# Turning q by the DMA crossbar instead of TensorE and VectorE

## The chip, the cores and the metric

The kernel runs on one core of one Trainium2 chip. The metric is the device time of one execution in microseconds (us). An execution more than 1.5% above the fastest of the same kernel counts as slow. Ratios use the fast ones alone; medians are over all executions.

SBUF is the memory on the chip that holds the tiles; PSUM, divided into banks, takes the results of TensorE here. DMA engines move data beside the computing engines, in packets. The granted clock is the share of TensorE's full clock that the profile reports.

## The reference, cut to what matters

```python
kv  = einsum('bhsd,bhse->bhde', k, v)            # per batch b and head h: 64 x 64
out = einsum('bhsd,bhde->bhse', q, kv)           # q: (8, 8, 576, 64)
out = out / sqrt(mean(out**2, -1) + 1e-6) * g_norm
x   = out.transpose(0, 2, 1, 3).reshape(4608, 512)
h   = x @ w_in                                   # (512, 1024)
solu = h * softmax(h)
ln  = (solu - mean) / sqrt(var + 1e-6) * g_ln    # over the 1024
result = ln @ w_out                              # (1024, 512)
```

`q @ kv` contracts over d, the last dimension of q. A matmul contracts over partitions, so q, which arrives with tokens on the partitions, has to be turned first. This turn is what the change is about.

## The kernel before

The work is cut into nine chunks of 512 tokens: chunks 0 to 7 hold 512 tokens of one batch each, chunk 8 the last 64 of all eight. Each engine gets a fixed order of instructions. A small list scheduler (`Plan.order`) finds it at build time: every piece of work is entered with its engine, an assumed length and its needs, and at each step the piece that could start first is taken. No order is written by hand.

The parts concerned (cuts are marked `...`):

```python
def load_q(b):                       # GpSimd's queue, casts f32 to bf16
    t = T["q", b] = tile_of(("q", b), [128, H, 4, D], BF16)
    nc.gpsimd.dma_start(...)

def qT_mm(c, hf, tag):               # half a chunk: 8 transposes into a PSUM bank
    t = T["qTp", c, hf] = bank((tag,), [128, 4, 2, 128], BF16)
    for h in range(4):
        for y in range(2):
            src = T["q", c][:, 4 * hf + h, 2 * y:2 * y + 2, :].rearrange("p z d -> p (z d)")
            nc.tensor.transpose(t[:, h, y, :], src, ident[:, :])

def qT_copy(c, hf):                  # and its evacuation
    t = T["qT", c, hf] = tile_of(("qT", c, hf), [128, 4, 2, 128], BF16)
    nc.vector.tensor_copy(t[:, :, :, :], T["qTp", c, hf][:, :, :, :])
...
def o_mm(c, hf, tag): ...            # o = kv' q', needs the turned q
def e_sum(c, n):                     # GpSimd: sum of two exponential tiles, 1.27 us
    ...
    nc.gpsimd.tensor_tensor(out=T["es", c][:, n, :], in0=e[:, 0, :], in1=e[:, 1, :], op=ADD)
...
def stats(c):                        # mean and variance of a chunk; tiny tiles
    nc.vector.tensor_copy(st[:, :, :], T["st", c][:, :, :])                       # from PSUM
    nc.vector.tensor_tensor(out=sq[:, :, :], in0=st[:, :, 1:3], in1=st[:, :, 1:3], op=MUL)
    nc.vector.tensor_tensor(out=var[:, :], in0=st[:, :, 0], in1=sq[:, :, 0], op=SUB)
    nc.vector.scalar_tensor_tensor(out=T["vare", c][:, :], in0=sq[:, :, 1], scalar=..., in1=var[:, :], op0=MUL, op1=ADD)
```

After o come its squares, their mean per head, logarithm and exponential, the product x, then h = x w_in (`h_ps` in the profile), u = h exp(h), the sums for the statistics, and the output matmuls (`out_ps`), which are scaled (`ob_sb`) and stored from SyncE's queue.

The softmax here doesn't subtract the row's maximum and nothing guards it: scores larger than these inputs give would overflow.

## Time and profile before

| | before |
|---|---|
| time, median (us) | 222.2 (4 runs, 220.6 to 223.0; 221.6 by the three known at the prediction) |
| span of the profiled execution | 218.7 |
| first h matmul | 23.15 |
| q of chunk 0 and 1 turned, first use in an o matmul | 15.18 and 30.34 |
| a steady chunk (from one chunk's turn of the sums to the next) | 19.90 |

TensorE is the fullest engine from 55 us on; before that, loads fill the DMA engines. The lines are in the prediction below. One more view, the time order of TensorE around the first use of the turned q in chunks 0 and 1 (start, us, engine, line, operation; in brackets the idle time before it and what ended it):

```profile
15.18 0.29 PE L274 MATMUL o_ps<-qT_sb,kvd 64*64 64x256 bf16 x1 [0.51 <-DVE kvd L247]
```

### The profile page before, as it was taken

How to read it: one execution, taken by the hardware profiler on the slowest of the kernel's cores; microseconds unless marked ns; L12 is line 12 of the kernel's file. 1: busy time of each engine (PE TensorE's matmuls, PEld its weight loads, DVE VectorE, ACT ScalarE, POOL GpSimd, SP SyncE). 2: the span in 40 equal slices, each digit the busy share in tenths (PEclk: the TensorE clock that was granted, in tenths of full speed). 3: DMA queues.
4: the chain of work that ended last, by engine and by line, in shares of the span. 5: the costliest groups of instructions: out<-in, count | busy, mean ns of one | idle time of the engine just before them, and what ended most of it. 6: DMA issues, size and time to landing. Idle time of an engine off the chain costs nothing.

```text
span 218.7 us, 4197 instructions
## 1 busy us (share of the span) xinstructions
PE 188.8 (86%) x1669; PEld 85.8 (39%) x1695; DVE 137.7 (63%) x249; ACT 133.8 (61%) x227; POOL 131.8 (60%) x136
## 2 busy tenths in 40 slices
PE   7669796588999989999998999899999999999900
PEld 2434343243553444344435444443453444344300
DVE  1326564896777596669648675966785675493240
ACT  2019577757866877784977679586849685342000
POOL 8606299529479727984695584468466477485000
PEclk9699999999999999999999999999999999999995
DMA  5999999994992697289719940311032022013023
GB/s 53 187 201 205 230 361 201 201 189 53 201 210 60 94 193 185 63 109 221 190 13 189 224 115 4 109 48 51 0 119 76 3 96 96 0 64 125 6 69 124
DMA packets 30483, 27.01 MB, mean 123 GB/s; under 512 B 2304, under 2 KB 24832, under 8 KB 30464
## 3 DMA queue, kind: packets, MB, share of 16 engines
q0 software_dynamic: 24112, 17.30, 52.1%
q1 hardware_dynamic: 6352, 9.44, 12.6%
q8 instruction: 13, 0.21, 0.4%
q14 instruction: 6, 0.05, 0.1%
HBM read 32.51 MB, written 9.44 MB: 192 GB/s over the span
## 4 chain that ended last, share of the span: by engine, by line
PE 63%; DVE 14%; ACT 9%; DMA 5%; issue 4%; POOL 1%; DVEq 1%; POOLq 0%; ACTq 0%
PE out_ps L487 24%; PE h_ps L365 23%; PE misc_ps L429 6%; DMA v_sb<-in_v_dram 5%; PE misc_ps L257 3%; PE s_ps L295 3%; PE o_ps L274 3%; DVE u_sb L380 3%; DVE x_sb L310 2%; DVE ob_sb L494 2%; DVE kvd L247 2%; DVE w_out_sb L478 2%; ACT lss_sb L299 2%; ACT e_sb L373 2%; ACT osq_sb L289 2%
## 5 line engine op out<-in xcount | busy, mean ns | idle before, releaser
L365 PE MATMUL h_ps<-x_sb,w_in_sb 128*128 128x512 bf16 x273 | 71.7, 379 | 5.1 <-DVE x_sb L310 3.1
L391 POOL TENSOR_TENSOR usq_sb<-u_sb 128x512 bf16<-128x512 bf16 x58 | 59.9, 1040 | 23.1 <-DVE u_sb L380 23.1
L373 ACT ACTIVATE e_sb<-h_ps,zero_t 128x512 f32<-128x512 f32 x72 | 49.2, 684 | 37.7 <-PE h_ps L365 35.7
L487 PE MATMUL out_ps<-w_out_sb,u_sb 128*128 128x512 bf16 x262 | 67.1, 380 | 2.4 <-DVE ob_sb L494 1.1
L397 POOL TENSOR_TENSOR es_sb<-e_sb 128x512 bf16<-128x512 f32 x36 | 45.7, 1269 | 37.4 <-ACT e_sb L373 37.3
L380 DVE TENSOR_TENSOR u_sb<-h_ps,e_sb 128x512 bf16<-128x512 f32 x72 | 48.9, 684 | 22.9 <-ACT e_sb L373 22.6
L365 PEld LDWEIGHTS <-w_in_sb 128*128 128x128 bf16 x288 | 26.4, 98 | 34.7 <-issue 7.7
L487 PEld LDWEIGHTS <-u_sb 128*128 128x128 bf16 x288 | 26.1, 98 | 34.5 <-issue 7.0
L494 DVE TENSOR_SCALAR ob_sb<-out_ps,rstd 128x512 f32<-128x512 f32 x34 | 24.9, 743 | 11.7 <-PE out_ps L487 10.2
L310 DVE SCALAR_TENSOR_TENSOR x_sb<-o_ps,g_rep,rst_sb 128x512 bf16<-128x512 f32 x34 | 25.4, 746 | 6.5 <-ACT rst_sb L303 6.4
L303 ACT ACTIVATE rst_sb<-lss_sb,zero_t 128x512 f32<-128x512 f32 x36 | 25.8, 722 | 0.6
L299 ACT ACTIVATE lss_sb<-s_ps,eps_t 128x512 f32<-128x512 f32 x34 | 23.2, 683 | 1.9 <-PE s_ps L295 1.9
L289 ACT ACTIVATE osq_sb<-o_ps,zero_t 128x512 bf16<-128x512 f32 x33 | 21.1, 684 | 3.7 <-PE o_ps L274 2.7
L249 ACT CAST kvd<-misc_ps 64x256 bf16<-64x256 f32 x16 | 5.9, 368 | 16.7 <-DVE kvd L247 16.3
L295 PE MATMUL s_ps<-osq_sb,head_mean 128*128 128x512 bf16 x34 | 12.9, 380 | 0.7 <-ACT lss_sb L299 0.7
L257 PE MATMUL misc_ps<-ident,q_sb 128*128 128x128 bf16 x120 | 9.5, 224 | 3.8 <-DMA q_sb<-in_q_dram 2.0
L257 PEld LDWEIGHTS <-q_sb 128*128 128x128 bf16 x128 | 8.8, 103 | 8.8 <-issue 3.5
L438 DVE STREAM_TRANSPOSE sumT_sb<-misc_ps 128x512 f32<-128x512 f32 x9 | 6.4, 713 | 9.1 <-PE misc_ps L429 9.1
L261 DVE COPY qT_sb<-misc_ps 128x1024 bf16<-128x1024 bf16 x17 | 11.6, 679 | 0.4 <-PE misc_ps L257 0.4
L389 ACT ACTIVATE usq_sb<-u_sb,zero_t 128x512 bf16<-128x512 bf16 x14 | 10.1, 722 | 2.6 <-DVE u_sb L380 2.6
L274 PE MATMUL o_ps<-qT_sb,kvd 64*64 64x32 bf16 (+1 forms) x248 | 8.7, 229 | 2.2 <-DVE kvd L247 1.1
L247 DVE CAST kvd<-misc_ps 64x256 bf16<-64x256 f32 x16 | 6.6, 414 | 5.3 <-PE misc_ps L238 3.0
(60 smaller groups left out, 133.0 us busy)
## 6 DMA issues: line engine op xcount, KB each, us to landing
out_dram<-ob_sb SPq DMA_DIRECT2D x36, 256.0 KB, 3.1
k_sb<-in_k_dram POOLq DMA_DIRECT2D x8, 576.0 KB, 7.3
v_sb<-in_v_dram POOLq DMA_DIRECT2D x8, 576.0 KB, 9.8
q_sb<-in_q_dram POOLq DMA_DIRECT2D x8, 512.0 KB, 12.6
w_out_f<-in_moe_w_out_dram POOLq DMA_DIRECT2D x1, 2048.0 KB, 26.1
w_in_sb<-in_moe_w_in_dram POOLq DMA_DIRECT2D x2, 512.0 KB, 13.8
q_last<-in_q_dram POOLq DMA_DIRECT2D x8, 64.0 KB, 3.1
g_rep<-in_g_norm_dram SPq DMA_DIRECT2D x2, 0.2 KB, 2.3
```

Of the source, the lines that this page charges most:

```text
L257: nc.tensor.transpose(t[:, h, y, :], src, ident[:, :])
L289: nc.scalar.activation(out=t[:, :], in_=T[("o", *i)].rearrange("p a b c -> p (a b c)"), func=AF.Square, bias=zero_t[:, :])
L299: nc.scalar.activation(out=t[:, :], in_=T["s", i][:, :], func=AF.Ln, bias=eps_t[:, :])
L303: nc.scalar.activation(out=t.rearrange("p a b c -> p (a b c)"), in_=T["lss", i][:, :], func=AF.Exp, scale=-0.5, bias=zero_t[:, :])
L310: nc.vector.scalar_tensor_tensor(out=T["x", c][:, 2 * hf:2 * hf + 2, z], in0=T["o", c, hf, z][:, :, :, :], scalar=g_rep[:, :], in1=T["rst" ...
L365: nc.tensor.matmul(t[:, :], w_in_sb[:, dt, f * 128:(f + 1) * 128], T["x", c][:, dt].rearrange("p a b c -> p (a b c)"), start=(dt == 0), st ...
L373: nc.scalar.activation(out=T["e", c, f // 2][:, f % 2, :], in_=T["h", c, f][:, :], func=AF.Exp, bias=zero_t[:, :])
L380: nc.vector.tensor_tensor(out=T["u", c][:, f, :], in0=T["h", c, f][:, :], in1=T["e", c, f // 2][:, f % 2, :], op=MUL)
L391: nc.gpsimd.tensor_tensor(out=dst, in0=src, in1=src, op=MUL)
L397: nc.gpsimd.tensor_tensor(out=T["es", c][:, n, :], in0=e[:, 0, :], in1=e[:, 1, :], op=ADD)
L487: nc.tensor.matmul(T["acc", c, m][:, :], T["u", c][:, f, m * 128:(m + 1) * 128], w_out_sb[:, f, :], start=(f == 0), stop=(f == NF - 1),)
L494: nc.vector.tensor_scalar_mul(out=t[:, :], in0=T["acc", c, m][:, :], scalar1=T["rstd", c][:, m:m + 1])
```

## The change

The intent is to free TensorE, the fullest engine, of 144 transposes and VectorE of 18 copies, by letting the DMA engines turn q from SBUF to SBUF. The core of the diff:

```diff
-            done[n] = t + length + (0.2 if engine == "pe" else 0.12)
+            done[n] = t + length + {"pe": 0.2, "sp": 1.5}.get(engine, 0.12)
...
-    plan.add("warm2", "pe", 2.6, -9.0, lambda: warm(12), [("qT_mm", 0, 1)], first=[("s", "warm2")])
+    plan.add("warm2", "pe", 5.2, -8.0, lambda: warm(24), ["warm"], first=[("s", "warm2")])
...
-    def qT_mm(c, hf, tag): ...
-    def qT_copy(c, hf): ...
+    def q_turn(c):
+        t = T["qT", c] = tile_of(("qT", c), [128, H, 2, 128], BF16)
+        nc.sync.dma_start_transpose(
+            t.rearrange("q h y p -> q (h y) p"), T["q", c].rearrange("p h j d -> p (h j d)")
+        )
...
+        plan.add(("qT", c), "sp", 2.2, r, lambda c=c: q_turn(c),
+                 [("q", c)] if c < B else [("q_last", b) for b in range(B)], ...)
```

The schedule is told that a turn takes 2.2 us on SyncE and is there 1.5 us later.

More of the change, by code (lines that the diff above doesn't have):

```diff
@@ L113 @@
     bufs = {
-        "k": 3, "v": 3, "q": 3, "qT": 4, "osq": 4, "lss": 2, "rst": 2, "oc": 2, "x": 2, "e": 4, "u": 2, "usq": 2, "es": 2,
+        "k": 3, "v": 3, "q": 3, "qT": 2, "osq": 4, "lss": 2, "rst": 2, "oc": 2, "x": 2, "e": 4, "u": 2, "usq": 2, "es": 2,
         "sumT": 2, "ob": 4,
@@ L249, in kv_copy @@
             nc.scalar.copy(dst, src)
-    def qT_mm(c, hf, tag):
-        t = T["qTp", c, hf] = bank((tag,), [128, 4, 2, 128], BF16)
-        for h in range(4):
-            for y in range(2):
-                src = T["q", c][:, 4 * hf + h, 2 * y:2 * y + 2, :].rearrange("p z d -> p (z d)")
-                nc.tensor.transpose(t[:, h, y, :], src, ident[:, :])
-    def qT_copy(c, hf):
-        t = T["qT", c, hf] = tile_of(("qT", c, hf), [128, 4, 2, 128], BF16)
-        nc.vector.tensor_copy(t[:, :, :, :], T["qTp", c, hf][:, :, :, :])
+    def q_turn(c):
[3 more added lines that the diff above has]
+        )
     def o_mm(c, hf, tag):
@@ L275, in o_mm @@
                             ts[z][hh * 64:hh * 64 + 64, pp, :, cols], kvd[rows, b, hh, 2 * hf + pp, :],
-                            T["qT", c, hf][rows, 2 * pp + hh, :, cols], start=True, stop=True,
+                            T["qT", c][rows, 4 * hf + 2 * pp + hh, :, cols], start=True, stop=True,
                         )
@@ L326 @@
         kvs = [("kv", b, hh, z) for b in ([c] if c < B else range(B)) for hh in range(2) for z in range(2)]
+        plan.add(("qT", c), "sp", 2.2, r, lambda c=c: q_turn(c),
+                 [("q", c)] if c < B else [("q_last", b) for b in range(B)],
+                 uses=[("q", c)] if c < B else [], first=[("qT", c)])
         for hf in range(2):
-            loads = [("q", c)] if c < B else [("q_last", b) for b in range(B)]
-            qtag = "h" if c == 0 and hf else "misc"
-            plan.add(("qT_mm", c, hf), "pe", 0.5, (r + w * (0.1 + 0.1 * hf)) if c else -2.0, lambda c=c, hf=hf, tag=qtag: qT_mm(c, hf, tag),
-                     ["ident", *loads], uses=[("q", c)] if c < B else [], first=[(qtag, "qT", c, hf)])
-            plan.add(("qT", c, hf), "dve", 0.62, (r + w * (0.12 + 0.1 * hf)) if c else -2.0, lambda c=c, hf=hf: qT_copy(c, hf),
-                     [("qT_mm", c, hf)], uses=[(qtag, "qT", c, hf)], first=[("qT", c, hf)])
             tag = "out" if c == 0 and hf else "o"
             plan.add(("o_mm", c, hf), "pe", 0.25 if c < B else 1.2, r + w * (0.35 + 0.5 * hf),
-                     lambda c=c, hf=hf, tag=tag: o_mm(c, hf, tag), [("qT", c, hf), *kvs],
-                     uses=[("qT", c, hf)], first=[(tag, c, hf, z) for z in range(2)])
+                     lambda c=c, hf=hf, tag=tag: o_mm(c, hf, tag), [("qT", c), *kvs],
+                     uses=[("qT", c)], first=[(tag, c, hf, z) for z in range(2)])
             for z in range(2):
```

## The prediction

> **What bounds the kernel now.** I read the engine totals first, then the 40 slices, then the chain that ended last, then the groups of the lines that the change touches, and last the chain inside one steady chunk.
>
> The totals and three rows of the slices (each slice is 5.47 us; a digit is tenths busy):
>
> ```profile
> PE 188.8 (86%) x1669; PEld 85.8 (39%) x1695; DVE 137.7 (63%) x249; ACT 133.8 (61%) x227; POOL 131.8 (60%) x136
> ...
> PE   7669796588999989999998999899999999999900
> ...
> DMA  5999999994992697289719940311032022013023
> ```
>
> TensorE is the fullest engine, and its row is at 8 or 9 from slice 11 (55 us) to slice 38. Before that it is at 5 to 9, while the DMA row is at 9. So there are two stages: a head of some 50 us, in which loads and latencies set the pace, and a long stage where TensorE does. The change must be judged in each.
>
> The chain that ended last, by engine, agrees:
>
> ```profile
> PE 63%; DVE 14%; ACT 9%; DMA 5%; issue 4%; POOL 1%; DVEq 1%; POOLq 0%; ACTq 0%
> ```
>
> Of this the turning of q on TensorE (line 257) has 2.7%, by the chain's list of lines: 0.027 x 218.7 = 5.9 us. These are the groups that go (mean ns of one, then idle before them):
>
> ```profile
> L257 PE MATMUL misc_ps<-ident,q_sb 128*128 128x128 bf16 x120 | 9.5, 224 | 3.8 <-DMA q_sb<-in_q_dram 2.0
> ...
> L261 DVE COPY qT_sb<-misc_ps 128x1024 bf16<-128x1024 bf16 x17 | 11.6, 679 | 0.4 <-PE misc_ps L257 0.4
> ```
>
> And this is the chain in the middle of one steady chunk (start, us, what), from the chunk that runs from 111.65 to 131.55 us:
>
> ```profile
> 118.36 0.43 DVE kvd L247
> 118.79 0.02 issue
> 118.81 0.38 ACT kvd L249
> 119.19 0.04 issue
> 119.23 0.61 PE misc_ps L257 x8
> 119.84 0.86 PE h_ps L365 x4
> 120.70 0.86 PE out_ps L487 x4
> 121.57 0.45 PE misc_ps L257 x8
> ```
>
> The reader is to see two things here. Eight transposes advance the chain by 0.45 us (56 ns each), although one is listed with 219 to 224 ns: they are pipelined, so their busy time is not their cost. And the first eight wait for the last evacuation of k'v (line 249). They write the "misc" bank, of which there is one, which k'v, both halves of the turned q and the sums of the statistics share. In the time order TensorE is idle 0.48 us before 119.23 for this.
>
> **What the skill says.** "TensorE: Matmul & The Clock Gate", "Wait — 56ns, not 53.3ns?", has 55.6 ns from start to start at N = 128 with a warm clock; the trace agrees (0.45 / 8 = 56 ns). "VectorE: DVE Perf Modes", "The three transpose paths", gives 1309 ns for one 128x128 bf16 tile by the DMA crossbar. "DMA: Bandwidth & Descriptors", "Latency and other measured facts", gives a transposing DMA 261 GB/s where the middle dimension is not contiguous, and 350 to 400 where it is. The kernel before has no such DMA, so its trace can't decide between them, and they are far apart for one turn of 128x2048 (512 KB, sixteen such tiles): 524,288 B / 261 GB/s = 2.0 us, but 16 x 1.309 = 20.9 us if tiles went one by one. The same page, "Queues, rings and completion order", says each DMA engine goes round-robin between queue rows, packet by packet. The trace fits: a 256 KB store on the SyncE queue lands in 3.1 us (median) and 6.4 at worst, amid loads that take 7 to 13.
>
> **The change, part by part.**
>
> 1. *TensorE loses 144 transposes* (9 chunks x 16). Per chunk 16 x 56 ns = 0.90 us of issue time. With it goes the 0.48 us wait for the "misc" bank, if nothing else fills that place: sums and k'v come at other times of the chunk. So 0.9 to 1.4 us per chunk where TensorE is the bound. That holds for the chunks whose q is turned after 55 us: chunks 3 to 7 and the last one (line 257 near 60, 80, 99, 119, 139 and 157 us), six in all. 6 x 0.9 = 5.4 and 6 x 1.4 = 8.3; I take 7 us. The steady chunks last 19.9 us, with 19.05 us listed as TensorE busy, 13.9 VectorE, 15.1 ScalarE and 14.5 GpSimd, so no other engine stops a chunk of 18.7.
>
> 2. *VectorE loses 18 copies* of 0.68 us, 12.2 us. In the steady stage it is 70% busy and its copies are beside other work: nothing more. In the head two of them lie in the chain (at 45.0 and 46.9 us, 0.60 each, between the w_out scalings): 1.2 us comes back there.
>
> 3. *SyncE gains nine issues*, one of 2.2 us by the schedule's own figure, with 1.5 us to landing. I take it as an estimate of the author's. The queue has only 36 stores (0.3 us each if nothing blocks them), so 9 x 2.2 us is no load. It is in order, though: a turn that waits for a late q holds up stores behind it. Four output buffers give those stores most of a chunk of slack.
>
> 4. *The DMA engines gain* nine moves of 512 KB inside SBUF. In the steady stage k, v, q and stores take their share for about half of a chunk, and q of chunk 7, issued at 114.3 us, is first used at 139: there is room for a turn of 4 to 8 us. In the head there isn't: asked for 5 to 50 us, the DMA view shows 9 in each slice but the last, and some 200 GB/s. Each of three turns there (chunks 0, 1 and 2) pushes the loads behind it back by its own length, 2.0 to 2.6 us (524,288 B at 261 and at 200 GB/s, an estimate).
>
> 5. *What that costs the head.* q of chunk 0 lands at 7.4 us and its turn would be there at about 11 to 14, while the first use of it is at 15.2, after k'v: not late by itself. But v of chunk 0, whose landing at 13.6 us is in the chain, comes up to 2 us later. q of chunk 1 lands at 28.0, where its first transposes start at once and the first half is turned by 29.5. With a DMA of about 5 us on top and 2 us of delay before, that is 35. The x of chunk 1 (now done at 42.8) doesn't slip by all of this, since ScalarE does the exponentials of chunk 0 in the meantime. w_out lands at 34.5 and would land at 38 to 39. Its eight scalings on VectorE follow, less the 1.2 us of part 2. I put the head at 2 to 3 us longer in all, with the clock warm-up (24 idle matmuls at the start in place of 12 there and 12 later) worth nothing either way.
>
> 6. *Buffers*: two for a whole turned q in place of four halves, the same bytes. A turn waits for the output matmuls of the chunk two before, which are over by then.
>
> Sum: -7 (part 1), -1 (part 2), +2.5 (part 5): about -5.5 us, 221.6 to **216 us** (0.975).
>
> **The rivals.**
> *The turn is slow.* If the tile figure of 1309 ns holds one by one, a turn takes 21 us, longer than a chunk, and the DMA becomes the bound: 9 x 21 = 190 us from the landing of q0, plus a last chunk, some 230 us or more. For it: the page's figure. Against it: that is one lone tile, most of which could be fixed latency, and the schedule's figures (2.2 + 1.5 us) look like measured ones. A milder form, 8 to 12 us when it alternates with loads, stays hidden in the steady stage and costs the head 5 us or more: no gain, 219 to 224.
> *Another wait comes in TensorE's place.* In the steady chunk the chain also runs through statistics, u, ob and k'v on VectorE and ScalarE (114.9 to 119.2 us). If those dependences and not TensorE's issue order set the chunk, the removal gives half: 219 us. Against it: TensorE was busy during that stretch but for the half microsecond before the transposes.
> *The head hides it all.* If v0 slips by nothing and q1 is turned in slack, the full 8 us show: 212 to 213.
>
> **Range and chances.** The middle case is 216. The best, with all of part 1 and a free head, is near 210; the milder slow turn gives 224. The 8-in-10 range is 210 to 225, wider upward since the turn's time is in no trace that I have. Faster by over 2% means under 217.2: 0.54. Within 2%: 0.26. Slower: 0.20, nearly all of it the first rival.
>
> **What would show it.** The profile of the changed kernel should list no line 257 or 261, about 144 fewer matmul records, VectorE busy near 125 us, steady chunks of 18.5 to 19.0 us, nine transposing DMAs with 4 to 8 us to landing, and the first h matmul (now 23.15 us) at 23 to 26. If TensorE waits for the turned q after 60 us, or stores pile up behind a turn, the first rival is right. If chunks stay near 19.9 with no such wait, the second is. The prediction is wrong most simply if landing takes over 10 us.

## More of the kernel before

```profile
30.34 0.41 PE L274 MATMUL o_ps<-qT_sb,kvd 64*64 64x256 bf16 x8
```

Neither waits for q: the first waits for k'v (kvd), the second for nothing.

## The result, and the profile after

The changed kernel takes 243.98 us (median of 4 runs, 242.9 to 246.2), the kernel before 222.17. The ratio is 1.100 (95% interval 1.090 to 1.111): **slower by 10%**. Ratios here are the mean time of one kernel's fast runs over that of the other's in the same rounds, so not quite the ratio of the medians. The result is correct.

The page of the changed kernel: totals, two rows of the 40 slices (6.03 us each), the chain that ended last by engine and by line, and one row of the DMA issues (count, then median us from issue to landing):

```profile
PE 190.7 (79%) x1538; PEld 81.1 (34%) x1563; DVE 130.0 (54%) x231; ACT 133.4 (55%) x227; POOL 131.8 (55%) x136
...
PE   8910787276978799999799899989969799999910
...
DMA  6999999999089956996976997045021103103113
...
PE 51%; DMA 22%; DVE 14%; ACT 4%; issue 3%; POOL 3%; DVEq 1%; POOLq 0%; ACTq 0%
PE out_ps L479 19%; PE h_ps L357 19%; DMA qT_sb<-q_sb 12%; DMA q_sb<-in_q_dram 10%; PE misc_ps L421 5%; DVE u_sb L372 3%; DVE x_sb L305 3%; DVE ob_sb L486 3%; PE o_ps L269 3%; PE s_ps L290 2%; DVE var L448 1%; ACT lss_sb L294 1%; PE misc_ps L238 1%; DVE kvd L247 1%; DVE vare L450 1%
...
qT_sb<-q_sb SPq DMA_TRANSPOSE x8, 4.4
```

The work is gone as planned: no transposes, VectorE 7.7 us less. TensorE's busy time nevertheless rose from 188.8 to 190.7. Two things that the page shows add to it: the warm-up has 12 more idle matmuls (2.6 us), and matmuls are longer while the clock is low (h matmuls 389 ns in the mean, before 379). The first slices of TensorE are emptier, and DMA went from 5% of the chain to 22%: 12% are turns and 10% the load of q of chunk 1. The median landing of 4.4 us looks harmless, and that is the trap: it is the steady stage's. The same views as above, for chunks 0 and 1:

```profile
25.51 0.64 PE L269 MATMUL o_ps<-qT_sb,kvd 64*64 64x256 bf16 x8 [9.64 <-DMA qT_sb<-q_sb]
```

```profile
47.25 0.64 PE L269 MATMUL o_ps<-qT_sb,kvd 64*64 64x256 bf16 x8 [4.41 <-DMA qT_sb<-q_sb]
```

And the chain between them (start, us, what):

```profile
7.45 24.12 DMA q_sb<-in_q_dram
31.57 0.02 issue
31.58 15.62 DMA qT_sb<-q_sb
47.21 0.04 issue
47.25 0.64 PE o_ps L269 x6
```

The turn of chunk 0 was issued at 7.79 us, when its q landed, and was there at 25.5: 17.7 us. The turn of chunk 1 took 15.6, and its q had landed at 31.57, 3.6 us later than before. So the first o matmuls came 10.3 us late, those of chunk 1 16.9 us late. The chain holds the load of q and the turn of chunk 1; the turn of chunk 0 is not in it, since TensorE, done with what that turn had delayed, still idled 4.41 us for chunk 1.

The turn of chunk 2, issued at 48.83 us, still has packets after 58, but TensorE does not wait for it. That of chunk 3 is the third to be waited for. It is in the chain too (first line), and TensorE idled 1.81 us for it (second line):

```profile
70.15 12.80 DMA qT_sb<-q_sb
```

```profile
83.00 0.41 PE L269 MATMUL o_ps<-qT_sb,kvd 64*64 64x256 bf16 x8 [1.81 <-DMA qT_sb<-q_sb]
```

The steady stage did not gain either. These are the windows of one chunk (stretch, its length, then busy us and instructions of TensorE, its weight loads, VectorE, ScalarE and GpSimd, clock, DMA share, GB/s), before and then after:

```profile
111.65:131.55 19.90, 19.05 (x177) 8.76 (x184) 13.91 (x26) 15.12 (x26) 14.53 (x16) 1.00 0.83 146
```

```profile
108.17:128.51 20.34, 18.65 (x162) 7.86 (x168) 13.73 (x24) 15.16 (x26) 14.55 (x16) 1.00 0.95 172
```

TensorE has less to do in the chunk, and the chunk is 0.44 us longer. So there are two questions: what the turns cost in the head, and what ate the gain in the steady stage.

### The profile page after: what moved, and what is told of

The parts are those of the page before. It is cut to its first block, busy times and chain, and to the rows that moved or that the text cites. A ratio compares the mean times of both kernels' runs of the same rounds, so it can differ in the third digit from the quotient of the medians.

```text
span 241.1 us, 3926 instructions
## 1 busy us (share of the span) xinstructions
PE 190.7 (79%) x1538; PEld 81.1 (34%) x1563; DVE 130.0 (54%) x231; ACT 133.4 (55%) x227; POOL 131.8 (55%) x136
## 4 chain that ended last, share of the span: by engine, by line
PE 51%; DMA 22%; DVE 14%; ACT 4%; issue 3%; POOL 3%; DVEq 1%; POOLq 0%; ACTq 0%
PE out_ps L479 19%; PE h_ps L357 19%; DMA qT_sb<-q_sb 12%; DMA q_sb<-in_q_dram 10%; PE misc_ps L421 5%; DVE u_sb L372 3%; DVE x_sb L305 3%; DVE ob_sb L486 3%; PE o_ps L269 3%; PE s_ps L290 2%; DVE var L448 1%; ACT lss_sb L294 1%; PE misc_ps L238 1%; DVE kvd L247 1%; DVE vare L450 1%
## 5 line engine op out<-in xcount | busy, mean ns | idle before, releaser
L357 PE MATMUL h_ps<-x_sb,w_in_sb 128*128 128x512 bf16 x272 | 73.5, 389 | 5.9 <-DVE u_sb L372 3.2
L479 PE MATMUL out_ps<-w_out_sb,u_sb 128*128 128x512 bf16 x264 | 70.3, 390 | 3.5 <-DVE ob_sb L486 2.6
L479 PEld LDWEIGHTS <-u_sb 128*128 128x128 bf16 x288 | 26.9, 99 | 40.4 <-issue 12.9
L486 DVE TENSOR_SCALAR ob_sb<-out_ps,rstd 128x512 f32<-128x512 f32 x34 | 25.2, 745 | 21.0 <-PE out_ps L479 16.9
L269 PE MATMUL o_ps<-qT_sb,kvd 64*64 64x32 bf16 (+1 forms) x248 | 9.7, 238 | 22.2 <-DMA qT_sb<-q_sb 15.9
L290 PE MATMUL s_ps<-osq_sb,head_mean 128*128 128x512 bf16 x34 | 13.7, 404 | 3.0 <-ACT lss_sb L294 2.0
L269 PEld LDWEIGHTS <-kvd 64*64 64x64 bf16 x256 | 4.9, 111 | 29.6 <-issue 22.0
L175 PE MATMUL s_ps<-zeros 128*128 128x512 bf16 x36 | 10.4, 457 | 1.3 <-DVE zeros L145 1.2
L280 POOL TENSOR_TENSOR osq_sb<-oc_sb 128x512 bf16<-128x512 f32 x1 | 1.0, 1038 | 17.8 <-DVE oc_sb L276 17.8
## 6 DMA issues: line engine op xcount, KB each, us to landing
w_in_sb<-in_moe_w_in_dram POOLq DMA_DIRECT2D x2, 512.0 KB, 15.6
```

The lines of the kernel that those rows point to most:

```text
L269: nc.tensor.matmul(ts[z][hh * 64:hh * 64 + 64, pp, :, cols], kvd[rows, b, hh, 2 * hf + pp, :], T["qT", c][rows, 4 * hf + 2 * pp + hh, :, c ...
L357: nc.tensor.matmul(t[:, :], w_in_sb[:, dt, f * 128:(f + 1) * 128], T["x", c][:, dt].rearrange("p a b c -> p (a b c)"), start=(dt == 0), st ...
L479: nc.tensor.matmul(T["acc", c, m][:, :], T["u", c][:, f, m * 128:(m + 1) * 128], w_out_sb[:, f, :], start=(f == 0), stop=(f == NF - 1),)
L486: nc.vector.tensor_scalar_mul(out=t[:, :], in0=T["acc", c, m][:, :], scalar1=T["rstd", c][:, m:m + 1])
```

## The experiments

Theory 1: the turn is slow because it shares the DMA engines with the loads of the head. Rival: the schedule's new order of work is what costs. A kernel has an order (that of before, or that of the change) and a way to turn q (TensorE, DMA, or none at all with a constant tile in its place). Experiments take the two apart. That orders were the same was checked on each computing engine, instruction group by instruction group in the time order, apart from the turning of q and what the table names.

The runs that were timed in several rounds, in one table. "Stats" is the start of VectorE's turn of the sums, one per chunk, a good milestone. The chunk length is from the stats of chunk 3 to those of chunk 4.

| run | order | q turned by | time, us | first h | stats 0 | chunk 3 to 4 | stats 8 |
|---|---|---|---|---|---|---|---|
| before | before | TensorE | 222.7 | 23.15 | 50.69 | 19.90 | 204.75 |
| the change | change | DMA | 244.0 | 33.52 | 63.90 | 20.34 | 227.33 |
| none_after_order | change | none | 225.5 | 25.45 | 49.94 | 20.33 | 210.59 |
| none_before_order | before | none | 217.1 | 25.48 | 52.65 | 18.93 | 201.75 |
| dma_before_order | before | DMA | 234.1 | 33.77 | 69.45 | 18.93 | 218.56 |
| head_by_pe | its own | TensorE 0-3, DMA 4-8 | 227.2 | 25.60 | 54.52 | 20.33 | 211.18 |
| head3_before_order | before | TensorE 0-2, DMA 3-8 | 217.7 | 23.45 | 51.77 | 18.93 | 200.89 |
| only_head_dma | before | DMA 0-1, TensorE 2-8 | 240.6 | 33.33 | 69.57 | 19.90 | 223.64 |
| none_warm | before | none | 215.9 | 23.62 | 50.80 | 18.92 | 199.92 |
| none_after_x_first | change, three pairs swapped | none | 225.5 | 24.52 | 50.71 | 20.33 | 211.36 |
| none_after_psum | change | none | 219.7 | 24.62 | 50.19 | 19.25 | 203.66 |
| after_psum | change | DMA | 241.3 | 34.62 | 64.62 | 19.25 | 225.88 |
| head3_psum | before | TensorE 0-2, DMA 3-8 | 215.7 | 24.91 | 53.38 | 18.93 | 200.15 |

Times are medians; that of before is from the rounds of the first four experiments (in other rounds 221.5 to 223.2). Rounds of different experiments ran on different chips, and the kernel before moved by 1.7 us between them, so differences across rounds are good to 1 or 2 us only. Without their one slow execution head3_before_order is at 217.4 and head3_psum at 215.5. The milestones are from the profiled execution, which for the kernel before was one of its fastest (220.5 us).

### Order and turn, taken apart

```diff
 # none_after_order: the changed kernel, wrong on purpose
+    q_const = big.tile([128, H, 2, 128], BF16, name="q_const")
+    nc.vector.memset(q_const, 0.05)
     def q_turn(c):
-        t = T["qT", c] = tile_of(...); nc.sync.dma_start_transpose(...)
+        T["qT", c] = q_const
```

> The changed kernel with its nine turns taken out and nothing in their place (o is computed from a constant tile, so the result is wrong on purpose); the order of work on every engine is that of the changed kernel, instruction for instruction. Theory 1 (the turn loses its time as a slow DMA among the loads of the head): the first h matmul is back at 22 to 24 us, against 33.5 with the turn, and the time is 211 to 219 us. Rival (the changed order of work costs most of it): the time stays at 230 us or above. Side question: if a steady chunk stays near 20.3 us, as with the turn, the steady stage is set by the order and not by the DMA; if it falls to 18.5 to 19, the DMA holds it.

It took 225.45 us, between the 211 to 219 of theory 1 and the 230 of the rival: each has a part. The head is nearly back (first h at 25.45, expected 22 to 24), but the steady chunk stays at 20.33 us. So the DMA does not hold the steady chunk; the order does.

```diff
 # none_before_order: the kernel before, wrong on purpose
     def qT_mm(c, hf, tag):
-        ... 8 transposes
+        pass
     def qT_copy(c, hf):
-        ... copy
+        T["qT", c, hf] = q_const
```

The scheduler still plans the empty pieces with their old lengths, so all other work keeps its order.

> The kernel before with its transposes and copies of q taken out and nothing in their place (constant tile, wrong on purpose); the order of all other work is that of the kernel before. It shows the most that part 1 and 2 of the prediction could give. If they were right: 212 to 215 us, steady chunks of 18.5 to 19.0 us in place of 19.9. Rival (a chain of dependences through VectorE and ScalarE holds the chunk, not TensorE's issue): 218 us or more, chunks of 19.5 or more.

217.14 us, ratio to before 0.975 (0.969 to 0.982), above the 212 to 215 expected and below the rival's 218. The steady chunk lost 0.97 us, as expected. Part of what is missing is the clock, as shown further below.

```diff
 # dma_before_order: as above, and
+        plan.add(("q_turn", c), "sp", 0.1, r - 1.0, lambda c=c: q_turn(c), ...)   # as soon as q is there
```

> The DMA turn, but with all other work in the order of the kernel before (three turned tiles, the turn issued as soon as q is there). Theory 1: the head loses as in the changed kernel, first h matmul at 32 to 35 us, and the time is 232 to 242 us. Rival (the changed order is what costs): 222 us or less.

234.05 us, ratio 1.051 (1.045 to 1.058), correct. Its steady chunk is the same as without any turn:

```profile
110.84:129.76 18.92, 18.16 (x158) 7.87 (x160) 12.63 (x23) 15.00 (x27) 14.55 (x16) 1.00 1.02 181
```

The whole cost of the turns in this order, 234.05 - 217.14 = 16.9 us, is there by the stats of chunk 0 (69.45 - 52.65 = 16.8) and doesn't grow after.

The four medians now give the account of the change: taking the work away -5.6 us (217.1 - 222.7), the new order +8.3 (225.45 - 217.14), the turns +18.5 (243.98 - 225.45, from different rounds). The milestones of the profiled executions agree in sign and rank at the stats of chunk 8: -3.00 + 8.84 + 16.74 = 22.58 us. The first is smaller there because the profiled execution of the kernel before was one of its fastest.

### Where the turns cost

> Chunks 0 to 3 are turned by TensorE and VectorE as before, chunks 4 to 8 by DMA as in the change; the order is the schedule's own for this mix. Theory 1: without turns among the loads of the head the loss is gone: first h matmul at 23 to 24 us, 215 to 224 us. Rival (the DMA turn costs everywhere, by blocked stores or by a slow steady stage): 228 us or more.

The edit enters the old pieces for chunks 0 to 3 and the new one for 4 to 8 and lets the scheduler find its own order. 227.20 us, ratio 1.022 (1.014 to 1.030). The first h matmul comes at 25.6 (23 to 24 expected), so the head's loss of ten microseconds is mostly gone, but the time is above the range expected: the chunk is again 20.33 us. The expectation had counted the turns and forgotten the order.

> Chunks 0 to 2 turned by TensorE as before, chunks 3 to 8 by DMA, all other work in the order of the kernel before. From the runs so far: the order of before costs nothing, a steady chunk loses 0.97 us by the turn and the head is that of before. Over chunks 3 to 8 this is 5 us: 215.5 to 218.5 us, faster than both kernels. Rival (turns cost something in the steady stage that the runs without them hide): 220 us or more.

```diff
 # head3_before_order: dma_before_order, and
+    HEAD = (0, 1, 2)
     def qT_mm(c, hf, tag):
+        if c not in HEAD:
+            return
         ... 8 transposes                       # likewise qT_copy; o_mm takes either tile
```

217.73 us, ratio 0.977 (0.971 to 0.983), correct, faster than both kernels. Its turns land in 4.5 to 6.0 us, and TensorE waits for none of them. The opposite mix:

> The opposite mix: only chunks 0 and 1, whose turns fall among the loads of the head, are turned by DMA, chunks 2 to 8 by TensorE as before; the order is that of the kernel before. If the head's two turns alone cost what the run with all turns lost against none (16.8 us, with 0.97 us per chunk not won back): 236 to 241 us, first h matmul at 33 to 34 us, steady chunks 19.9 us. Rival (the loss needs the later turns too): below 232 us.

`HEAD = (2, 3, 4, 5, 6, 7, 8)` gives 240.63 us, ratio 1.084 (1.077 to 1.092), with the stats of chunk 0 at 69.57 and the old chunk of 19.90 us. Two turns, those of chunks 0 and 1, are enough for the whole loss of this order: 18.9 us at the stats of chunk 0 (against the run without any turn, which is itself 2.0 us later there than the kernel before, 16.9). No run separates the two; the chain of this one, too, holds the turn of chunk 1 (15.5 us) and not that of chunk 0. In the changed order the turn of chunk 3 comes on top.

### Why a turn in the head is slow

```diff
 # quiet_turn: the changed kernel, in load_q(0)
+        turn_now(0)
+        nc.gpsimd.tensor_copy(held_t[:, :], T["qT", 0][:, H - 1, 1, 127:128])   # GpSimd waits for the turn
```

> The changed kernel, but GpSimd reads one element of the first turned tile before it issues any load other than that of q of chunk 0. So the first turn runs on empty DMA engines, and all later loads start some 9 us later. Theory 1 (a turn is slow only because its packets alternate with those of the loads): the first turn lands 4 to 5 us after its issue, in place of 17.7. Rival (the first turn is slow of itself, or because it is first): it stays above 10 us. The total is no test here, since the loads start late; 236 to 250 us.

The time, one look, was 249.9 us, as the loads start late. The first turn landed in 4.4 us. This is the DMA view of the 4.5 us around it (queue: packets, MB, share of the 16 engines' time; then the issue, us to landing):

```profile
q1 hardware_dynamic: 2080, 0.52, 61.3%
...
qT_sb<-q_sb SPq DMA_TRANSPOSE x1, 4.4
```

And the same turn in the changed kernel, from 8 to 24 us, beside the loads (q0):

```profile
q0 software_dynamic: 3059, 2.56, 100.6%
q1 hardware_dynamic: 2068, 0.50, 24.7%
```

A turn is 2080 packets, 0.52 MB, so some 250 bytes each. Alone they move at some 215 GB/s. Beside the loads they need until 25 us, and the loads move five times as many bytes in the 16 us shown. The turn is not slow of itself; beside the loads it gets a sixth of the bytes.

> The changed kernel with each turn issued as two of half the size (four pairs of heads each), into two tiles. If the turn's packets alternate with the loads' packets one by one, landing grows with the number of packets: the first half of chunk 0 lands 8 to 10 us after its issue and the second near 17.7. If instead the turn stands in a line behind the loads issued before it, both halves land together, at 16 us or later. The time is 238 to 245 us, as x of chunk 0 needs both halves.

Each turn was issued as two halves into two tiles. One look: 237.5 us (state unknown). TensorE's first uses of the halves:

```profile
19.77 0.64 PE L270 MATMUL o_ps<-qTh_sb,kvd 64*64 64x256 bf16 x8 [3.20 <-DMA qTh_sb<-q_sb]
...
26.99 0.64 PE L270 MATMUL out_ps<-qTh_sb,kvd 64*64 64x256 bf16 x8 [6.59 <-DMA qTh_sb<-q_sb]
```

The first half landed 11.9 us after its issue, the second 7.2 us after the first (17.7 after its own issue). So the turn does not stand in one line behind all earlier loads, or both would have come together. Nor is 11.9 within the 8 to 10 us of the other theory: the landing grows with the packets, on top of a few microseconds. I then tried to find the rule by which the engines share.

> The changed kernel, with the first turn run beside a known load: GpSimd issues q of chunk 0, then w_out and w_in with their rows of 2048 bytes as before, and holds all other loads until the turn has landed. From the quiet turn (130 packets on each of 16 engines, some 20 ns each, and 1.8 us fixed) and about 110 ns for a load packet of 2 KB: if the engine takes one packet of the turn and one of the load in turns, 1.8 + 130 x (20 + 110) ns = 18.7 us, less where the loads run out before (96 packets each engine, at 14 us). So 12 to 19 us. Rival (shares by bytes or by time, half each): 7 to 8 us, whatever the packet size.

> The same bytes beside the first turn, but w_out and w_in are read in pieces of 512 bytes, four times as many packets of about a quarter of the time each (some 30 ns). Packet by packet: 1.8 + 130 x (20 + 30) ns = 8.3 us, so 7 to 11 us, clearly less than beside packets of 2 KB. Rival (shares by bytes or time): the same landing time in both runs.

Both let the first turn run beside w_out and w_in alone, in rows of 2048 bytes and in pieces of 512. The landing was 14.2 us and 12.4:

```profile
qT_sb<-q_sb SPq DMA_TRANSPOSE x1, 14.2
```

```profile
qT_sb<-q_sb SPq DMA_TRANSPOSE x1, 12.4
```

The first lies in the range of "one packet each in turns", the second does not (7 to 11), and neither lies at the 7 to 8 us of equal shares. The landing times alone don't give the rule. The packet counts of a stretch in which both queues are at work do. This is the DMA view of the changed kernel from 16 to 20 us, then of the two runs from 16 to 18 us, beside_2k first:

```profile
q0 software_dynamic: 625, 0.62, 91.4%
q1 hardware_dynamic: 625, 0.16, 29.9%
```

```profile
q0 software_dynamic: 318, 0.31, 91.3%
q1 hardware_dynamic: 317, 0.08, 30.1%
...
q0 software_dynamic: 675, 0.17, 82.3%
q1 hardware_dynamic: 676, 0.17, 64.7%
```

One packet of the turn goes with one packet of the loads, whatever its size: the bytes are as one to four where a load packet is counted with 1.0 KB, and equal where it has 250 bytes. Equal shares of the bytes would not give this. A pair takes 102 ns on each of the 16 engines in the changed kernel (4 us / 39), 101 in beside_2k and 47 in beside_512, where 130 and 50 had been assumed.

The second term is the start. Alone the turn's packets begin 1.2 us after its issue (by the slices of the DMA view of quiet_turn). In the changed kernel none is seen before 12 us, over 4 us after it; in beside_2k and beside_512 they begin some 4.5 and 5 us after it. An estimate from these: 4.4 + 130 x 0.102 = 17.7 us, as measured. Why the start is later beside loads stays open; the expectation for beside_512 missed it.

### Why the matmuls of the head were late even with no turn

Without turns the first h matmul still came at 25.5 us, not 23.15. The kernel before had 12 idle matmuls after its transposes, up to 12.7 us; the experiment issues them earlier and then idles until v lands.

> The kernel before without transposes and copies, as in the run with the order of before, but with 34 in place of 12 idle matmuls in the second warm-up, so that TensorE stays busy until v of chunk 0 lands at about 13.6 us. If the first h matmul came at 25.5 us in place of 23.15 only because the clock had fallen in the idle time from 9.5 to 14 us, it is back at 23 to 24 us here and the time is 1.5 to 2.5 us less than 217.1. Rival (something else delays it): no change, 25.5 us and 217 us.

```diff
-    ... lambda: warm(12), [("qT_mm", 0, 1)]
+    ... lambda: warm(34), [("qT_mm", 0, 1)]
```

The k'v matmuls of chunk 0, without and with the longer warm-up:

```profile
14.23 1.49 PE L238 MATMUL misc_ps<-v_sb,k_sb 96*64 96x64 bf16 x48 [4.74 <-DMA v_sb<-in_v_dram]
```

```profile
14.20 0.95 PE L238 MATMUL misc_ps<-v_sb,k_sb 96*64 96x64 bf16 x48
```

The same 48 matmuls take 1.49 us at a granted clock of 0.50 (14 to 15 us) and 0.95 at 1.00. The first h matmul is at 23.62 again and the time 215.91 us (ratio 0.969, 0.965 to 0.974), 1.2 us less than without (a little short of the 1.5 to 2.5 expected). So part of what the transposes did, together with the idle matmuls behind them, was to keep TensorE's clock up.

### What the new order costs in the steady chunk

The chain of a steady chunk in the new order has an x product between u and the first output scaling, which TensorE awaits for 0.85 us. The first idea was this place.

> As the run without turns in the changed order (225.45 us, steady chunk 20.34 us; wrong on purpose), with one pair of VectorE instructions swapped in each of three steady chunks: the x product before the u product after the statistics, so that VectorE does x in the 0.62 us in which it waits for the exponential, as the order of before does. If this place sets the longer chunk, TensorE's wait of 0.85 us for the first ob goes and the three chunks fall by 0.6 to 0.9 us each, the time by about 2 us, to 223.5 us. Rival (the order costs elsewhere, the swap only moves the wait): chunks of 20.2 us or more, no change.

Three pairs were swapped in the order found. Result: 225.50 us, chunks of 20.34 us, no change. The idea fell. VectorE had not been idle before u, as I had taken from the chain's "issue" of 0.62 us; a look at the time order of VectorE and GpSimd (from none_after_order) shows what it did:

```profile
118.84 1.25 DVE L449 SCALAR_TENSOR_TENSOR vare<-sq,var 128x4 f32<-128x4 f32 x1
```

```profile
118.81 1.26 POOL L388 TENSOR_TENSOR es_sb<-e_sb 128x512 bf16<-128x512 f32 x1 [0.57 <-ACT e_sb L364]
```

The last of the small statistics instructions, on 128x4 elements, takes 1.25 us where it usually takes 0.16 (median), and it ends with a GpSimd addition that began 0.03 us before it. The Trainium skill has this: "SBUF — State Buffer", "SBUF: two separate sides", says that VectorE and GpSimd share a port pair as an exclusive lock, which a VectorE instruction with two SBUF inputs needs against a GpSimd instruction that reads SBUF, and that the later one blocks. `vare` reads sq and var, both in SBUF. In the order of before it starts at 114.93 us in its chunk, 0.43 before the GpSimd addition at 115.36, and takes 0.16. The test takes the second SBUF input away:

```diff
-        nc.vector.tensor_tensor(out=sq..., in0=st[:, :, 1:3], in1=st[:, :, 1:3], op=MUL)
+        nc.vector.tensor_tensor(out=sq..., in0=st[:, :, 1:3], in1=T["st", c][:, :, 1:3], op=MUL)
-        var = small.tile([128, 4], FP32, name="var")
+        var = T["st", c][:, :, 0]            # the variance goes back into its PSUM bank
-        nc.vector.tensor_tensor(out=var[:, :], in0=st[:, :, 0], in1=sq[:, :, 0], op=SUB)
+        nc.vector.tensor_tensor(out=var, in0=T["st", c][:, :, 0], in1=sq[:, :, 0], op=SUB)
```

> The run without turns in the changed order (225.45 us, steady chunk 20.34 us; wrong on purpose), with the statistics written so that none of their small VectorE instructions has two SBUF inputs (the variance goes back into its PSUM bank). In that run the last of them took 1.25 us instead of 0.16 in each of three steady chunks, beginning just after the GpSimd addition of 1.26 us began. Theory (the two lock each other out, and the changed order brings them together): the instruction takes 0.2 us everywhere, the steady chunks fall to 19.2 to 19.5 us, the time to 220.5 to 223 us. Rival (the long record only shows another wait): chunks stay at 20.3 us.

The two instructions meet as before, and the small one is short:

```profile
114.39 1.27 POOL L388 TENSOR_TENSOR es_sb<-e_sb 128x512 bf16<-128x512 f32 x1 [0.58 <-ACT e_sb L364]
114.43 0.16 DVE L449 SCALAR_TENSOR_TENSOR vare<-sq,misc_ps 128x4 f32<-128x4 f32 x1
```

The chunk fell to 19.25 us, as expected, and the time to 219.74, 5.7 us less than without this edit by the medians. The two ran in different rounds; by their ratios to the kernel before (1.013 and 0.994) the gain is some 4.4 us (an estimate: 0.0196 x 222). So of the 8.3 us that the new order costs, 4 to 6 are such collisions. The rest stays open. The order of before has them too: there the same instruction is long in two chunks.

> The changed kernel, turns and all, with the statistics as in the run above. Theory: the same gain as without the turns, steady chunks of 19.2 to 19.5 us, 238 to 241 us in place of 244. Rival: no change, 243 to 245 us.

241.26 us, just above the range (ratio 1.088, 1.078 to 1.097); the chunks are at 19.25. With the turns the same edit gives 2.7 us, less than without them; the profiled execution loses part of it between the stats of chunks 0 and 1 (31.3 us against 28.1). There TensorE waits 5.85 us for the turn of chunk 3 at 84.19 us, against 1.81 in the changed kernel. Why that turn is later still, no run isolates.

> The best mix so far (chunks 0 to 2 by TensorE, 3 to 8 by DMA, order of before: 217.7 us) with the statistics as above. There the instruction is long in two chunks and near the end. Theory: up to 1 us from each that lies in the chain: 215 to 217 us. Rival: 217.5 us or more.

215.73 us, ratio 0.974 (0.968 to 0.979), correct: **the lowest time of a correct version**, 2.6% faster than the kernel before. The expected range was 215 to 217. Its lead over head3_before_order, 2 us of medians, is not shown: the rounds differ, and the intervals of the two ratios overlap (0.968 to 0.979 and 0.971 to 0.983).

## Why the prediction was wrong

**What bounds the kernel** was right: a head of loads and latencies, then TensorE.

**Part 1, TensorE's transposes: right with the order held fixed.** It gave 0.9 to 1.4 us a chunk; none_before_order shows 0.97. The wait of 0.48 us for the "misc" bank gave hardly anything beyond that: in the order of before, TensorE now waits about 0.4 us for u in the same stretch instead. The whole removal is worth 5.6 us, or 6.8 with the warm-up mended (222.7 - 215.9), where the prediction had 8 (so the "full 8 us" of its third rival would be 213.6, a little above its "212 to 213", and its best case, 221.6 - 8.3 - 1.2 = 212.1, was not "near 210").

**Part 3, SyncE: right where it counts.** The issues took 1.3 to 3 us in quiet stretches, near the 2.2 assumed, and up to 7.8 us beside loads; they held no store that shows in the order of before (the chunk is 18.93 with turns and without).

**Part 4, the turn's own length: right, and its use wrong.** I had estimated 2.0 to 2.6 us of moving for 512 KB; quiet_turn shows 0.52 MB at some 215 GB/s, 2.4 us, and 4.4 to landing. I also was right that the steady stage has room: in head3_before_order every turn lands in 4.5 to 6.0 us. But in the changed order the turn of chunk 3 met loads at 70 us and took 12.8.

**Part 5 is the step that failed.** It read "its turn would be there at about 11 to 14, while the first use of it is at 15.2" and "I put the head at 2 to 3 us longer in all". Measured: 25.5 us, and 16.8 us longer with the order held fixed. I had added the turn's length to the queue, as if an engine served it fully and then went on. I had quoted that engines alternate packet by packet, and did not carry it into the sum: 130 small packets on each engine, each behind a load packet, and a start over 4 us late. That made 17.7 us for chunk 0, and 15.6 for chunk 1 in place of "a DMA of about 5 us". The delay of v of chunk 0 held ("up to 2 us later", measured 1.2 by the start of its first matmul); w_out landed at 37.4 us for "38 to 39"; but q of chunk 1 came 3.6 us later in place of "2 us of delay before". And the slack that I granted x of chunk 1 was not there: ScalarE ran out of work of chunk 0 before the turn landed (it idled 4.4 us for the o matmuls at 47.25).

**A term was missing.** The sum had no line for the order of work. The scheduler moves everything when a piece goes, and the order that it found costs 8.3 us without any turn, of which 4 to 6 are small VectorE instructions meeting GpSimd ones. "So no other engine stops a chunk of 18.7" was argued from busy times, which can't show this.

**Part 2** is not settled apart from part 1; VectorE's busy time fell by 7.7 us and not by the 12.2 of the copies. Part of the difference is the statistics: their three tiny instructions per chunk that work from SBUF take 10.9 us in all after the change, 7.8 before. **The warm-up** "worth nothing either way" was wrong: in none_before_order the lower clock cost 1.2 us.

**The rivals.** The first, in its "milder form, 8 to 12 us when it alternates with loads", was the right kind of mistake to fear, but put at "5 us or more" for the head and 219 to 224 in all. It went wrong in size: 12.8 to 17.7 us for the three turns that TensorE waited for. Its sign, TensorE waiting for a turn after 60 us, was seen once (1.81 us at 83.00). The second (another wait in TensorE's place) fails with the order held fixed, where the chunk fell by 0.97 us; in the changed order its sign, chunks that stay, was there, through a collision that it did not name. In the chances, slower got 0.20.

## What to carry to other kernels

Before work is moved to the DMA engines, ask what else is in their queues at the moment when the result is awaited: the same transfer took 4.4 us alone and 17.7 beside loads, and its own length is only a lower bound. Count packets, not bytes: here one went for one, and those of the turn were small. So use the idle stretch for it (here chunks 3 to 8, with the order of before) and keep the old path in the crowded one. And where a scheduler finds the order, test the change with the order held fixed, and look for small instructions that are suddenly long: they may show a collision that the totals hide.

## What the Trainium skill lacked or had wrong

- "DMA: Bandwidth & Descriptors", "Queues, rings and completion order": it says that engines go round-robin by packets, and the trace agrees (625 packets of each queue from 16 to 20 us). But no page says what a transposing DMA gets beside loads by this. Here: packets of some 250 bytes, 0.16 MB against 0.62 in those 4 us, a start over 4 us after the issue in place of 1.2, and landing in 17.7 us against 4.4 alone. "Rules for kernel authors" there says that a transpose next to ordinary DMAs needs nothing; the results here were indeed correct, but it needs time.
- "VectorE: DVE Perf Modes", "The three transpose paths": its 1309 ns is for one tile of 128x128, and the page doesn't say what several in one DMA take; it must not be multiplied. Sixteen such tiles in one DMA landed in 4.4 us, 0.28 us each. The 261 GB/s of "DMA: Bandwidth & Descriptors" was nearer: some 215 while moving.
- "TensorE: Matmul & The Clock Gate", "What's actually happening", lets the clock fall after an idle window of about 3.4 us. In the kernel before, TensorE was idle only from 5.4 to 7.4 us, 2.0 us, and the granted clock of the stretch from 8 to 9 us was 0.50.
